# A transform, mix and two-MLP kernel: a buffer each for normalised, turned and read-back tokens, with chunk sizes, preparations, read-backs, decode pieces and the first channel transforms in another order

## The chip, the core and the metric

The kernel runs on one NeuronCore of a Trainium2 chip. Time is device time in microseconds (us) of one execution; lower is better. The engines are PE (TensorE, matrix products), DVE (VectorE), ACT (ScalarE), POOL (GpSimd) and SP (SyncE, which here only issues DMAs, one after the other, in one queue that keeps its order). Each engine runs its own instructions in order; semaphores tie the engines together.

## What is computed

Two sequences of 3136 tokens with 256 channels go through three layers. Cut to what matters:

```python
# 1: filter along the sequence
X  = rfft(x, axis=1)
Yr = Xr @ w_r - Xi @ w_i + b_r;  Yi = Xr @ w_i + Xi @ w_r + b_i
Y  = soft_threshold(Yr, 0.01) + 1j * soft_threshold(Yi, 0.01)
x  = irfft(Y, axis=1)
# 2: MLP1 (256 -> 1024 -> 256)
xn = (x - mean(x)) / sqrt(var(x) + 1e-6) * g_ln
x  = x + relu(xn @ w_ch1) @ w_ch2
# 3: Fourier mixing, then MLP2 of the same size with weights of its own
u  = x + real(fft(fft(x, axis=1), axis=2))
un = (u - mean(u)) / sqrt(var(u) + 1e-6)
out = u + relu(un @ w2_ch1) @ w2_ch2
```

## The kernel before

Every product is made of split operands: a value is taken apart into a high and a low part, and two or three matmuls of `fp32r` add up to one product (`mm3r`, lines L223 to L225).

**Layer 1.** Forward transforms, the channel product per frequency (`p2_mix`, L483) and the inverse transform. The last part of the inverse (class `Inverse`) runs in 16 steps per sequence: DVE turns a piece (L321), PE multiplies it (L323), ACT copies it out of PSUM into `yg` (L205). After the sixteenth step of a sequence seven DMAs write `yg` to `dY` in memory (L329, L331), and the token loads of MLP1 read it back (L595). The steps of the second sequence run as hooks inside the first chunks of MLP1.

**MLP1 and MLP2** are 13 chunks each, `mlp1[0..12]` and `mlp2[0..12]`, of up to four tiles of 128 tokens; chunks of sequence 0 come first. What one chunk needs, in its order:

- load: tokens from memory into `yb` (or, for the first ones, `u0r` or `stg`), L595;
- stats: mean and variance of each tile on DVE (L605, L606);
- norm: the root on ACT (L613), four small DVE operations (L614 to L617), then per tile two ACT passes (L627 subtracts the mean, L628 scales) into `yn`;
- flip: two DVE transposes of 32x32 blocks into `z` (L640), one DMA that writes `z` to `dT` in memory (L646) and one that reads it back channel by channel into `xt` (L649);
- trans: ACT and DVE split `xt` into the high and low operand in `u0r` (L664, L205, L213); `mlp1[0]` and `mlp1[1]` turn their tokens on PE instead (L672, split by L675 and L676);
- l1: for each of eight groups f of 128 hidden channels six matmuls (L223 to L225) into one of three PSUM buffers `psa`, which ACT empties with a relu (L690) and DVE with the low part (L692);
- l2: per tile 16 matmuls (L708, L709) into one of two buffers `psb`, two DVE additions (L712, L713) and a store (L721).

`yn`, `z` and `xt` all come from one pool "q" of three buffers that goes round in order of request: whoever asks next gets the buffer that was asked for three requests ago, and waits for its last reader.

**Layer 3's transform** stands between the two MLPs. Stage 4 (`Stage98`, matmuls on L223 to L225 into `psc`, ACT copies out, POOL L372 to L374, L213, L427) reads `dX` (L353), and writes `dA` (L428) in 16 steps per sequence: those of sequence 0 run as hooks in MLP1's chunks 8 to 10, those of sequence 1 in MLP2's chunks 1 to 3. The channel transform of an MLP2 chunk (class `Front`) loads pieces of `dA` (`r<-dA`, L756, L758), multiplies them (`stage_b`, L772), and `dmix` (from L797 on) adds the result to the token tile. `mlp2[6]` is the first that needs sequence 1 of `dA`.

**The order of the work.** `run_mlp` walks through the chunks. Around chunk k it puts, at numbered places ("l1" behind group f, "l2" behind tile i), the preparation of the next chunks: trans of k+1, stats, norm and flip of k+2, the loads of k+3 at its end, and the hooks: inverse steps, stage 4 steps, and eight pieces in which DVE decodes MLP2's weights (`MLP2_AT`). The tables at the head of the file give the places. On top of this a scheduler orders the instructions of each engine by durations of its own, within what the data allow, so that work can stand earlier or later than its place. Each DMA also waits for the DMA eight issues before it, since eight semaphores are used in turn.

Of the kernel before, what the change touches and what calls it, by code (L numbers as in the profile page):

```python
# [9 lines left out]
F32 = mybir.dt.float32  # L10
# [15 lines left out]
MLP2_AT = ((4, 6), (5, 2), (5, 6), (6, 2), (6, 6), (7, 3), (11, 2), (11, 6))  # L26
# [11 lines left out]
TRANS_AT = (0, 0)  # L38
# [18 lines left out]
D = 256  # L57
# [108 lines left out]
def fourier_moe_kernel(ctx, tc, x, w_r, w_i, b_r, b_i, g_ln, w11, w12, w21, w22,  # L166
# [415 lines left out]
    class Chunk:  # L582
# [3 lines left out]
        def __init__(self, nt, loads, stores, wv, g, front=None):  # L586
            self.nt, self.loads, self.stores, self.wv, self.g, self.front = nt, loads, stores, wv, g, front
            self.by_act = False
            self.flipped = True

        def load(self):
            self.y = next(y_ring).rearrange("p (i c) -> p i c", c=D)
# [3 lines left out]
            if self.front is not None:  # L596
                self.front.load()
# [10 lines left out]
        def norm(self):  # L608
# [9 lines left out]
            self.yn = qslot(F32).rearrange("p (i c) -> p i c", c=D)  # L618
# [15 lines left out]
        def flip(self, h):  # L634

            x = self.nt * 32
            if h == 0:
                self.z = qslot(F32)
# [9 lines left out]
            self.xt = qslot(F32)  # L648
# [3 lines left out]
        def trans(self, c):  # L652
            nt = self.nt
            n = nt * 128
            if c == 0:
                self.xh, self.xl = ((next(x_ring) if self.flipped else qslot()).rearrange("p (k c) -> p k c", k=2)
                                    for _ in range(2))
# [57 lines left out]
        def store(self, last):  # L715

            for ps_, i, n, ap in self.stores:
                if i + n - 1 != last:
                    continue
                s = self.o[ps_, i:i + n, :]  # L720
                sp.dma_start(out=ap, in_=s if n > 1 else s[:, 0, :])  # L721
# [3 lines left out]
    def chunks1(b, wv):  # L725
        cs = []
        if b == 0:
            plan = [(c * 512, 4) for c in range(6)]
        else:
            plan = [(64, 2), (320, 2)] + [(576 + c * 512, 4) for c in range(5)]  # L730
        for k, (r0, nt) in enumerate(plan):
            lo = [(ALLP, 0, nt, rows(dY[b], r0, 128, nt))]
            st = [(ALLP, 0, nt, rows(dX1[b], r0, 128, nt))]
            if b == 1 and k == 0:
# [182 lines left out]
    for i in range(NS + INV_BEHIND):  # L917
# [9 lines left out]
        if i == PREP0_AT[0]:  # L927
            with tc.high_priority(offset=100):
# [3 lines left out]
        if i == PREP0_AT[1]:  # L932
            for c in range(2):
# [4 lines left out]
    def run_mlp(chunks, nxt, hooks):  # L938

        allc = chunks + nxt  # L940
        for k, ch in enumerate(chunks):
# [3 lines left out]
            def put(part, i, f, *a):  # L945
# [5 lines left out]

            if n is not None and n.flipped:
                for c in range(2):
                    put("l2", TRANS_AT[c], split, c)
# [3 lines left out]
            for n_ in todo:  # L958
                if n_ is None:
                    continue  # L960
                two = n_.front is not None
                if two:
                    i = 0
                    for p, pr in enumerate(n_.front.pairs):
                        put("l1", STAGE_B_AT[p], n_.front.stage_b, p)
                        put("l1", DMIX_AT[p], n_.front.dmix, p, n_.y, i)
                        w = 2 if pr[0][1] else 1
                        for t in range(w):
                            put("l1", STATS2_AT[p], n_.stats, i + t)
                        i += w  # L970
                else:
                    def stats(t, ch=ch, n_=n_):
                        with ExitStack() as es:
                            if ch is mlp1[0]:
                                es.enter_context(tc.issue_after(ch.rest[STATS1_AT[t]]))
                            n_.stats(t)

                    for t in range(4):
                        put("l1", STATS1_AT[t], stats, t)
                put("l1", NORM_AT[two], n_.norm)  # L980
                if n_.flipped:
                    for h in range(2):
                        put("l2", FLIP_AT[h], n_.flip, h)
                else:
                    for c in range(2):
                        put("l2", ch.nt - 1, n_.trans, c)
# [9 lines left out]
            if far is not None:  # L996
                far.load()

    u0 = cp.tile([128, 8192], F32R, tag="u0", name="u0r")
    x_ring = ring(u0[:, 4096:8192], 4, 1024)  # L1000
# [94 lines left out]
```

## Time and profile before

| | |
|---|---|
| time, median of 3 runs | 821.51 us (818.88 to 823.38) |
| the profiled execution | 819.17 us, span 817.4 us |
| PE busy | 791.3 us (97%), 4276 matmuls |
| PE weight loads (beside the matmuls) | 658.9 us |
| DVE busy | 538.9 us (66%) |
| ACT busy | 364.1 us (45%) |
| POOL busy | 120.2 us (15%) |
| DMA | 95.16 MB, mean 116 GB/s |
| granted PE clock | 0.992 |

A line of the timeline gives start, duration, engine, line, operation, output <- input, how many instructions in a row it stands for, and in brackets the idle time of the engine before it and what ended it. Matmuls overlap, so their durations are longer than their distance. A window line gives an engine's busy time with its number of instructions, the granted PE clock (1.00 is full speed), and the share and rate of the DMA engines. The time of the profiled execution is 1.77 us longer than its span.

### The profile page before, as it was taken

What the parts mean: (1) busy time and instruction counts of PE and PEld (TensorE: products, weight loads), DVE (VectorE), ACT (ScalarE), POOL (GpSimd) and SP (SyncE); (2) the same over time, 40 slices, a digit from 0 to 9 for tenths busy, and PEclk for the clock granted to TensorE, in tenths of its full rate; (3) what the DMA queues carried; (4) which work ended last, traced back from release to release, by engine and by line L of the source; (5) the groups of instructions that cost most, each with busy time, mean ns of one, the idle gap of its engine ahead of it and who ended that gap; (6) DMA issues with size and microseconds to landing.
All of it is one profiled execution on the core that took longest, in us unless ns stands there. A gap on an engine that the chain in (4) does not pass through costs nothing.

```text
span 817.4 us, 12025 instructions
## 1 busy us (share of the span) xinstructions
PE 791.3 (97%) x4276; PEld 658.9 (81%) x4276; DVE 538.9 (66%) x1260; ACT 364.1 (45%) x791; POOL 120.2 (15%) x152
## 2 busy tenths in 40 slices
PE   9999999998999999989999999999979999999996
PEld 3888977966777888978788888888768898888885
DVE  6589996478557568976756874646535666666543
ACT  1422356356764444364442563555533444444321
POOL 1212221220000000025420002555300000000000
PEclk9999999999999999999999999999989999999999
DMA  8742200621177123464544135455352344322201
GB/s 231 218 134 86 78 1 2 211 105 54 51 226 218 65 78 129 163 167 150 172 163 129 64 105 155 137 157 165 100 142 78 101 137 122 93 67 79 69 23 33
DMA packets 79663, 95.16 MB, mean 116 GB/s; under 512 B 16610, under 2 KB 58858, under 8 KB 79408
## 3 DMA queue, kind: packets, MB, share of 16 engines
q1 hardware_dynamic: 79604, 94.40, 37.8%
q8 instruction: 34, 0.56, 0.3%
q14 instruction: 25, 0.20, 0.1%
HBM read 56.89 MB, written 37.49 MB: 115 GB/s over the span
## 4 chain that ended last, share of the span: by engine, by line
PE 76%; DMA 9%; DVE 8%; ACT 3%; SPq 2%; issue 1%; POOL 1%; ACTq 0%; POOLq 0%
PE psb L708 20%; PE psb L709 10%; PE psa L223 10%; PE psa L224 10%; PE psa L225 9%; PE psb L483 4%; PE psc L772 3%; PE psc L323 2%; PE psc L304 2%; PE psc L503 2%; PE psc L797 1%; DMA cb<-in_cb_dram 1%; PE psa L451 1%; DMA h<-in_x_dram 1%; DMA r<-dA 1%
## 5 line engine op out<-in xcount | busy, mean ns | idle before, releaser
L690 ACT ACTIVATE h<-psa 128x512 fp32r<-128x512 f32 (+2 forms) x208 | 116.3, 570 | 199.8 <-PE psa L225 157.0
L692 DVE SCALAR_TENSOR_TENSOR h<-psa,h 128x512 fp32r<-128x512 f32 (+2 forms) x208 | 134.4, 654 | 91.5 <-ACT h L690 89.9
L708 PE MATMUL psb<-r3a,h 128*128 128x512 f32 x392 | 137.5, 399 | 0.6 <-DVE o L713 0.6
L708 PE MATMUL psb<-r2b,h 128*128 128x512 f32 x392 | 137.7, 398 | 0.0
L709 PE MATMUL psb<-r2b,h 128*128 128x256 f32 x392 | 106.0, 281 | 0.0
L709 PE MATMUL psb<-r3a,h 128*128 128x256 f32 x392 | 105.9, 282 | 0.0
L483 PE MATMUL psb<-wm,h 128*128 128x256 f32 (+1 forms) x600 | 88.8, 298 | 0.9 <-DVE w L489 0.9
L708 PEld LDWEIGHTS psb<-r3a,h 128*128 128x128 f32 x392 | 71.6, 188 | 16.8 <-issue 1.5
L708 PEld LDWEIGHTS psb<-r2b,h 128*128 128x128 f32 x392 | 71.9, 188 | 14.7
L483 PEld LDWEIGHTS psb<-wm,h 128*128 128x128 f32 (+1 forms) x600 | 76.1, 189 | 8.7 <-issue 8.2
L223 PE MATMUL psa<-u0r,r2b 128*128 128x512 f32 (+2 forms) x208 | 81.9, 394 | 0.0
L224 PE MATMUL psa<-u0r,r2b 128*128 128x512 f32 (+2 forms) x208 | 80.0, 385 | 0.0
L225 PE MATMUL psa<-u0r,r2b 128*128 128x512 f32 (+2 forms) x208 | 79.6, 384 | 0.0
L709 PEld LDWEIGHTS psb<-r3a,h 128*128 128x128 f32 x392 | 73.7, 189 | 4.5 <-issue 0.7
L709 PEld LDWEIGHTS psb<-r2b,h 128*128 128x128 f32 x392 | 73.9, 189 | 3.2
L712 DVE TENSOR_TENSOR o<-psb,yb 128x256 f32<-128x256 f32 x74 | 30.6, 422 | 69.2 <-PE psb L709 68.4
L223 PE MATMUL psa<-u0r,r3a 128*128 128x512 f32 (+2 forms) x176 | 67.1, 382 | 4.0 <-DVE h L692 4.0
L205 ACT ACTIVATE yg<-psc 98x512 f32<-98x512 f32 (+2 forms) x58 | 48.4, 863 | 47.2 <-PE psc L503 27.2
L224 PE MATMUL psa<-u0r,r3a 128*128 128x512 f32 (+2 forms) x176 | 66.2, 376 | 0.0
L225 PE MATMUL psa<-u0r,r3a 128*128 128x512 f32 (+2 forms) x176 | 63.8, 380 | 0.0
L213 POOL TENSOR_TENSOR h<-w 128x512 f32<-128x512 f32 (+1 forms) x26 | 34.1, 1314 | 109.9 <-DVE w L490 76.4
L225 PEld LDWEIGHTS psa<-u0r,r2b 128*128 128x128 f32 x208 | 40.0, 192 | 7.7
(125 smaller groups left out, 1306.7 us busy)
## 6 DMA issues: line engine op xcount, KB each, us to landing
dT<-q SPq DMA_DIRECT2D x20, 512.0 KB
q<-dT SPq DMA_DIRECT2D x20, 512.0 KB
s<-in_moe_w_ch_dram SPq DMA_DIRECT2D x16, 512.0 KB
r<-dX SPq DMA_DIRECT2D x32, 196.0 KB
dA<-o SPq DMA_DIRECT2D x32, 196.0 KB
dY<-yg SPq DMA_DIRECT2D x12, 512.0 KB
r<-dA SPq DMA_DIRECT2D x48, 128.0 KB
dX<-o SPq DMA_DIRECT2D x11, 512.0 KB
```

Of the source, the lines that this page charges most:

```text
L205: nc.scalar.activation(out=o, in_=i, func=AF.Copy, scale=scale)
L213: ins = eng.tensor_tensor(out=o, in0=a, in1=b, op=ALU.subtract)
L223: nc.tensor.matmul(out=ps, lhsT=lh, rhs=rh, start=first, stop=False)
L224: nc.tensor.matmul(out=ps, lhsT=ll, rhs=rh, start=False, stop=False)
L225: ins = nc.tensor.matmul(out=ps, lhsT=lh, rhs=rl, start=False, stop=last)
L483: nc.tensor.matmul(out=ps[0:m, u * D:(u + 1) * D], lhsT=xv[:, o:o + m], rhs=wm_hl[wv][:, e, c, :], start=k == 0, stop=k == 11)
L690: ins = nc.scalar.activation(out=h[:, 0:n], in_=ps[:, 0:n], func=AF.Relu)
L692: ins = nc.vector.scalar_tensor_tensor(out=l[:, 0:n], in0=ps[:, 0:n], scalar=0.0, in1=h[:, 0:n], op0=ALU.max, op1=ALU.subtract)
L708: nc.tensor.matmul(out=ps, lhsT=h[:, ts_], rhs=w2[:, f, :], start=f == 0, stop=False)
L709: nc.tensor.matmul(out=ps[:, 0:D], lhsT=l[:, ts_], rhs=w2[:, f, 0:D], start=False, stop=f == NF - 1)
L712: nc.vector.tensor_tensor(out=o, in0=ps[:, 0:D], in1=self.y[:, i, :], op=ALU.add)
L772: nc.tensor.matmul(out=ps, lhsT=self.raw[p][0:n, k, q * 128:(q + 1) * 128], rhs=self.cols(n, pr[k][1], im), start=True, stop=True)
```

## The change

1. `yn`, `z` and `xt` have a fixed buffer each (`q_tiles[0..2]`) instead of the next one of the pool; the pair of operands of `mlp1[0]` and `mlp1[1]` moves from the pool to `u0r`.
2. The read-back `q<-dT` is a step of its own, `land`: for `mlp1[2]` and MLP2's chunks it comes in the next chunk behind l1 group 3, and on SP behind the last store of the chunk before; for the other chunks of MLP1 (`EARLY`) behind l2 tile 2.
3. Chunk sizes of MLP1, in tiles: before 4,4,4,4,4,4 and, for sequence 1, 3 (two plus a half of each sequence),2,4,4,4,4,4; after 4,4,4,4,2,4,3 and 4,4,4,4,4,4.
4. Stats, norm and flips of MLP1 chunks are put earlier; the channel transforms and preparations of `mlp2[0]` and `mlp2[6]` later (`LATE`); the decode piece of chunk 7 goes to chunk 12; the token loads of chunk k+3 come at the start of chunk k instead of its end (except `mlp1[6]`'s).

No arithmetic is added or taken away.

```diff
-MLP2_AT = ((4, 6), (5, 2), (5, 6), (6, 2), (6, 6), (7, 3), (11, 2), (11, 6))
+MLP2_AT = ((4, 6), (5, 2), (5, 6), (6, 2), (6, 6), (11, 2), (11, 6), (12, 3))
-STAGE_B_AT = (1, 3)
-DMIX_AT = (3, 5)
-STATS1_AT = (0, 1, 2, 3)
-STATS2_AT = (4, 6)
-NORM_AT = (4, 7)
-FLIP_AT = (1, 2)
+EARLY = {"stats": (("l1", 0), ("l1", 0), ("l1", 1), ("l1", 1)), "norm": ("l1", 2), "flip": (("l1", 5), ("l1", 6)),
+         "land": ("l2", 2)}
+LATE = {"b": (4, 6), "mix": (6, 7), "stats": (("l1", 7), ("l2", 0)), "norm": ("l2", 0), "flip": (("l2", 2), ("l2", 3))}
+LAND_AT = ("l1", 3)
...
-            self.yn = qslot(F32).rearrange("p (i c) -> p i c", c=D)
+            self.yn = q_tiles[0].rearrange("p (i c) -> p i c", c=D)
...
             if h == 0:
-                self.z = qslot(F32)
+                self.z = q_tiles[1]
...
-            self.xt = qslot(F32)
+            self.d = d
+
+        def land(self):
+            x, d = self.nt * 32, self.d
+            self.xt = q_tiles[2]
             sp.dma_start(out=self.xt[:, 0:8 * x].rearrange("p (i x) -> p i x", i=8),
                          in_=bass.AP(d.tensor, d.offset, [[x, 128], [128 * x, 8], [1, x]]))
...
-            plan = [(c * 512, 4) for c in range(6)]
+            plan = [(0, 4), (512, 4), (1024, 4), (1536, 4), (2048, 2), (2304, 4), (2816, 2)]
         else:
-            plan = [(64, 2), (320, 2)] + [(576 + c * 512, 4) for c in range(5)]
+            plan = [(64 + c * 512, 4) for c in range(6)]
...
             if n is not None and n.flipped:
+                if not n.landed:
+                    put(LAND_AT, land, n, allc[k - 1].sent if k else None)
...
+                    pl = LATE if n_ in (mlp2[0], mlp2[6]) else USUAL
...
+            soon = far is not None and far is not mlp1[6]
+            if soon:
+                far.fetch()
```

What the scheduler makes of it is seen at three places. In these rows an engine's instructions stand in their order; L numbers of the changed kernel are a few lines off those before.

DVE, end of MLP1's chunk 0, before: the end of the transposed preparation of `mlp1[1]` (L676), the additions of chunk 0's tiles (L712, L713), and the low parts `h` of chunk 1's l1 groups (L692).

```order
L676 SCALAR_TENSOR_TENSOR q<-psc,g_sb,q 128x512
L712 TENSOR_TENSOR o<-psb,stg 128x256
L713 TENSOR_TENSOR o<-psb,o 128x256
L321 STREAM_TRANSPOSE t_2107<-yg_85 128x512
L692 SCALAR_TENSOR_TENSOR h<-psa,h 128x512 x2
```

The same place now: L643 is the flip, two transposes for a chunk; the first pair is that of `mlp1[2]`, the second that of `mlp1[3]`.

```order
L683 SCALAR_TENSOR_TENSOR u0r<-psc,g_sb,u0r 128x512
L643 STREAM_TRANSPOSE q<-q 128x4x4x32 x2
L719 TENSOR_TENSOR o<-psb,stg 128x256
...
L719 TENSOR_TENSOR o<-psb,stg 128x256
L720 TENSOR_TENSOR o<-psb,o 128x256
L643 STREAM_TRANSPOSE q<-q 128x4x4x32 x2
L699 SCALAR_TENSOR_TENSOR h<-psa,h 128x512 x2
```

The flip of `mlp1[3]` has come ahead of chunk 1's low parts, and those of `mlp1[4]` and `mlp1[5]` follow between them; all write the one `z`, so each waits until the DMA of the one before has read it.

PE, MLP1's chunk 1, before: the sixteenth inverse step of sequence 1 (L323) stands behind three l1 groups of chunk 2 and ahead of the l2 of chunk 1's tiles 2 and 3.

```order
L225 MATMUL psa<-u0r,r3a 128x512 x3
L323 MATMUL psc<-t_2493,cim 98x512
L708 MATMUL psb<-r3a,h 128x512
L709 MATMUL psb<-r3a,h 128x256
```

Now it is the second L322 of these rows, with the fifteenth ahead of it; the rows above them are the end of two tiles' l2 and one l1 group of the next chunk.

```order
L715 MATMUL psb<-r3a,h 128x512
L716 MATMUL psb<-r3a,h 128x256
L222 MATMUL psa<-u0r,r3a 128x512
...
L224 MATMUL psa<-u0r,r3a 128x512
L322 MATMUL psc<-t_2333,cim 98x512
L322 MATMUL psc<-t_2475,cim 98x512
```

The last two inverse steps have moved behind 32 matmuls of l2 and six of l1.

SP, MLP2's chunk 2 to 3, before: `r_5863` is the last input of stage 4.

```order
L646 DMA dT_1657<-q 128x2x512
L428 DMA dA_71<-o_1661 98x512
L595 DMA yb<-dX_68 64x256
L721 DMA out_dram<-o 64x256 x2
L649 DMA q<-dT_1657 128x8x128
L595 DMA yb<-dX_69 64x256
L595 DMA yb<-dX_69 128x1x256
L721 DMA out_dram<-o 2x64x256
L428 DMA dA_71<-o_1661 98x512
L353 DMA r_5863<-dX_69 98x512
```

The same place now, where the last input is `r_5816`.

```order
L649 DMA dT_1657<-q 128x2x512
L427 DMA dA_71<-o_1661 98x512
L600 DMA yb<-dX_68 64x256
L728 DMA out_dram<-o 64x256 x2
L600 DMA yb<-dX_69 64x256
L600 DMA yb<-dX_69 128x1x256
L728 DMA out_dram<-o 2x64x256
L427 DMA dA_71<-o_1661 98x512
L656 DMA q<-dT_1657 128x8x128
L352 DMA r_5816<-dX_69 98x512
```

The read-back has moved behind two token loads, a store and a write of `dA`, and still stands ahead of the last input. On PE the first matmuls of `mlp2[6]`'s `stage_b` stand where they stood, behind the l2 of two tiles and nine matmuls of l1.

## Rows read from the trace of the kernel before

**Rows 1.** Waits of PE: line, releaser, us in total, times, longest.

```profile
PE psc L772 <- DMA r<-dA: 4.8, 2, 4.3
PE psa L223 <- DVE h L692: 4.0, 4, 1.9
PE psc L672 <- ACT yg L205: 2.4, 1, 2.4
PE psc L225 <- POOL u0r L213: 1.7, 1, 1.7
...
PE psc L218 <- POOL mhl L213: 0.5, 1, 0.5
PE psc L217 <- POOL mhl L390: 0.5, 1, 0.5
```

**Rows 2.** Windows: start:end, length, PE, PEld, DVE, ACT, POOL, PEclk, DMA, GB/s.

```profile
300.00:320.00 20.00, 20.00 (x104) 17.04 (x104) 15.54 (x31) 7.96 (x16) 0.00 (x0) 1.00 0.29 107
...
440.00:460.00 20.00, 20.00 (x113) 17.31 (x112) 19.50 (x58) 10.47 (x25) 0.00 (x0) 1.00 0.16 55
...
600.00:620.00 20.00, 15.67 (x71) 13.00 (x69) 5.95 (x12) 4.49 (x9) 0.00 (x0) 0.83 0.53 155
```

**Rows 3.** Timeline of ACT, end of chunk 0.

```profile
189.51 4.33 ACT L628 ACTIVATE q<-q,sm 128x256 f32<-128x256 f32 x8 [0.22 <-DVE sm L617]
```

**Rows 4.** Timeline of SP: two writes of dT and their read-backs.

```profile
195.60 0.39 SPq L646 DMA_DIRECT2D dT<-q  x1
198.55 0.37 SPq L649 DMA_DIRECT2D q<-dT  x1
...
252.77 0.48 SPq L646 DMA_DIRECT2D dT<-q  x1
260.79 0.37 SPq L649 DMA_DIRECT2D q<-dT  x1
```

**Rows 5.** Timelines of ACT and PE around 240 and 264 us.

```profile
239.10 1.31 ACT L627 ACTIVATE q<-u0r,ng 128x256 f32<-128x256 f32 x3 [3.54 <-issue]
...
242.87 0.50 PE L223 MATMUL psa<-u0r,r3a 128*128 128x512 f32 x1 [1.88 <-DVE h L692]
...
264.18 0.50 PE L223 MATMUL psa<-u0r,r3a 128*128 128x512 f32 x1 [0.81 <-DVE h L692]
```

**Rows 6.** Timelines of ACT, SP and DVE: sequence 1 of dY and its loads.

```profile
231.35 1.10 ACT L205 ACTIVATE yg<-psc 98x512 f32<-98x512 f32 x1 [0.59 <-PE psc L323]
...
243.33 1.45 SPq L649 DMA_DIRECT2D q<-dT  x1
...
253.79 1.08 DVE L605 BATCH_NORM_STATS2 st<-yb 128x6 f32<-128x256 f32 x3 [3.53 <-DMA yb<-dY]
...
258.21 0.43 DVE L605 BATCH_NORM_STATS2 st<-yb 128x6 f32<-128x256 f32 x1 [0.21 <-DMA yb<-dY]
```

**Rows 7.** Timeline of PE, first l1 groups of MLP1's chunk 8.

```profile
361.04 0.50 PE L223 MATMUL psa<-u0r,r3a 128*128 128x512 f32 x1 [1.16 <-DVE h L692]
```

**Rows 8.** Timelines of SP, POOL, ACT and PE: end of stage 4.

```profile
576.50 0.39 SPq L649 DMA_DIRECT2D q<-dT  x1
...
578.89 2.58 SPq L428 DMA_DIRECT2D dA<-o  x1
581.57 0.72 SPq L353 DMA_DIRECT2D r<-dX  x1
...
589.05 0.73 POOL L372 TENSOR_TENSOR w<-r 98x254 f32<-98x254 f32 x1 [11.46 <-DMA r<-dX]
...
593.67 1.70 ACT L628 ACTIVATE q<-q,sm 128x256 f32<-128x256 f32 x4
595.26 1.06 ACT L205 ACTIVATE o<-psc 98x512 f32<-98x512 f32 x2
...
604.25 1.05 SPq L756 DMA_DIRECT2D r<-dA  x2
...
610.41 1.08 PE L772 MATMUL psc<-cb,r 128*128 128x64 f32 x4 [4.33 <-DMA r<-dA]
```

More of the change, by code (lines that the diff above doesn't have):

```diff
@@ L589, in __init__, with fetch @@
             self.flipped = True
+            self.landed = False
         def load(self):
+            self.fetch()
+            if self.front is not None:
+                self.front.load()
+        def fetch(self):
             self.y = next(y_ring).rearrange("p (i c) -> p i c", c=D)
@@ L655, in trans @@
             if c == 0:
-                self.xh, self.xl = ((next(x_ring) if self.flipped else qslot()).rearrange("p (k c) -> p k c", k=2)
+                self.xh, self.xl = (next(x_ring).rearrange("p (k c) -> p k c", k=2)
                                     for _ in range(2))
@@ L720, in store @@
                 s = self.o[ps_, i:i + n, :]
-                sp.dma_start(out=ap, in_=s if n > 1 else s[:, 0, :])
+                ins = sp.dma_start(out=ap, in_=s if n > 1 else s[:, 0, :])
+                self.sent = getattr(ins, "ins", ins)
     ALLP = slice(0, 128)
@@ L727, in chunks1 @@
         if b == 0:
[L728 removed]
+            plan = [(0, 4), (512, 4), (1024, 4), (1536, 4), (2048, 2), (2304, 4), (2816, 2)]
         else:
[L730 to L731 removed]
+            plan = [(64 + c * 512, 4) for c in range(6)]
+        for r0, nt in plan:
             lo = [(ALLP, 0, nt, rows(dY[b], r0, 128, nt))]
             st = [(ALLP, 0, nt, rows(dX1[b], r0, 128, nt))]
[L734 removed]
+            if r0 == 2816:
                 for src, lst in ((dY, lo), (dX1, st)):
@@ L927, in fourier_moe_kernel @@
         if i == PREP0_AT[0]:
+            q_tiles = [qslot(F32) for _ in range(3)]
             with tc.high_priority(offset=100):
@@ L943, in run_mlp, with put @@
             at = {}
-            def put(part, i, f, *a):
+            def put(when, f, *a):
+                part, i = when
+                if part == "n":
+                    carry.append((("l1", i), f, a))
+                    return
                 at.setdefault((part, min(i, ch.nt - 1) if part == "l2" else i), []).append(lambda: f(*a))
@@ L950, in split, with land @@
                     n.trans(c)
+            def land(n, back):
+                with ExitStack() as es:
+                    if back is not None:
+                        es.enter_context(tc.issue_after(back))
+                    n.land()
+            for when, f, a in carried:
+                put(when, f, *a)
+            carried, carry = [], []
             if n is not None and n.flipped:
+                if not n.landed:
+                    put(LAND_AT, land, n, allc[k - 1].sent if k else None)
                 for c in range(2):
-                    put("l2", TRANS_AT[c], split, c)
+                    put(("l2", 0), split, c)
             todo = [m]
@@ L996, in run_mlp @@
             if far is not None:
-                far.load()
-    u0 = cp.tile([128, 8192], F32R, tag="u0", name="u0r")
-    x_ring = ring(u0[:, 4096:8192], 4, 1024)
+                if not soon:
+                    far.fetch()
+                if far.front is not None:
+                    far.front.load()
     dT = [dp.tile([2, 65536], F32, name=f"dT{i}") for i in range(3)]
```

34 lines of the change are left out of this document (20 added, 14 removed).

## The prediction

> **What bounds the kernel now.** The page's first part comes first: PE is busy 97% of the span, and the time is that of its matmuls plus what PE waits. The change takes no matmul away, so it can only move waits. The waits of PE are read next [rows 1]: the reader is to see how short the list is, and that every entry belongs to one of four places. One is the transposed preparation of `mlp1[1]` (2.4, L672). The second is the l1 groups of the following chunks (L223, 4.0 in four waits). The third is the end of sequence 0's stage 4 input (0.5 and 0.5, L217 and L218, with 1.16 of L223 just behind). The fourth is the end of stage 4 of sequence 1 (1.7 and 4.3, L225 and L772). Windows say the same: 20.00 of 20 us where nothing is missing, 15.67 in 600:620, with a granted clock of 0.83 there [rows 2]. The clock's two levels are 1.2 and 2.4 GHz, so 0.83 over 20 us means 6.8 us at the lower one, which costs 3.4 us beside the wait itself. The average share of the other engines (DVE 66%) says nothing here; each place is read from its own chain.
>
> From 300:320 comes a price that serves below: 104 matmuls in 20 us without a gap, 0.19 us each in the mix of l1 and l2 [rows 2].
>
> **Chunks 0 to 3 of MLP1.** The 2.4 us at L672 are a wait for ACT's copy of `yg`, which stood behind eight L628 in one go, 4.33 us [rows 3], because the norms of two chunks ran together. In the changed order only `mlp1[1]`'s norm stands ahead of these transposes, since `yn` is one buffer and `mlp1[2]`'s norm has to wait for them. That takes four L628 (2.2 us) and four L627 of 0.44 (1.8 us, by the three of 1.31 in [rows 5]) from the chain: 4.0, more than the wait. It goes: -2.4.
>
> In chunks 2 and 3 a norm stood at the head of ACT, waiting for a "q" buffer that a DMA was still reading, with the relus queued behind it: ACT idle 3.54 ahead of L627, then PE idle 1.88, later 0.81 [rows 5]. With buffers of their own and norms put early this waiting goes: -1.88 -0.81, and 0.15 for the fourth of L223's waits (4.0 less 1.88, 0.81 and the 1.16 of [rows 7]). Together with L672: -5.2.
>
> Two things come in. First, one `z`: the flips of `mlp1[3]`, `[4]` and `[5]` stand on DVE ahead of or between chunk 1's low parts, each waiting until the write of the flip before has read `z`. PE waits for the low parts, since they empty `psa`. A write took 2.95 us by the issue of the read-back behind it (195.60 to 198.55) [rows 4]. Ahead of the first of these waits lie a norm (four times 0.44 and 0.54, 3.9) and that write, 6.9 us and two flips on top; PE has meanwhile 32 matmuls of l2 and three l1 groups, 50 times 0.19, 9.6 us. So it is nearly covered; the later two have only what PE holds in three buffers (18 times 0.19, 3.5) against the same 2.95 and the work between. The bounds are 0 and three whole writes, 8.9. I take 2.
>
> Second, the last inverse step of sequence 1 moves behind 32 matmuls of l2 and six of l1, 38 times 0.19, 7.3 us. PE gets there 0.4 earlier (2.4 less 2), so the last copy of `yg`, 231.35 before [rows 6], comes at about 238.2. Behind it SP writes `dY` and loads the tokens of the next chunks. One thing that stood between goes, the read-back at 243.33 of 1.45 us; the tokens come 5.5 us later. Before, DVE waited 3.53 for the first of these (253.79) and had the third load at 258.21 [rows 6]; now that is about 263.7. In the changed order the statistics of three of these chunks stand on DVE ahead of chunk 3's first low part, and those are not done before 265. PE would have been at the fourth l1 group at 263.4 (264.18 less 0.81, [rows 5]), now 2.4 earlier, at 261. That makes a wait of 4, and one more when the last load follows: 5. Bounds: 0, if the writes go faster without the other traffic, and 8, the shift of 5.5 and the 2.4 that PE is ahead. The sum of this place: -5.2 +2 +5 = +1.8, from -5.2 to +11.7.
>
> **Chunks 6 to 8.** The middle of sequence 0's stage 4 input still follows chunk 6 (three tiles in both). Chunk 7 has four tiles instead of two, so PE has more work ahead of L217: two tiles of l2 alone are 32 times 0.19, 6.1 us, against waits of 0.5, 0.5 and then 1.16 [rows 1, 7]. -2.2; bounds 0 and -2.2. What is next late there is nothing that I can see.
>
> **Decode pieces.** One goes from chunk 7 to 12, beside MLP2's first preparations. In the window that holds two pieces DVE was busy 19.50 of 20, and PE lost nothing (20.00) [rows 2]. Chunk 12 becomes as full; half a microsecond of slack is no cover for a late load. +0.5, between 0 and 3. The shorter wait of L772 (4.8 less 4.3 [rows 1]) may go with the later place of `mlp2[0]`'s transforms: -0.3, between 0 and -0.5.
>
> **End of stage 4.** SP stood at the read-back until 576.50, then issued token loads, a store, a write of `dA` that held it from 578.89 on, and only then, at 581.57, the last `r<-dX`; POOL began on it at 589.05 after 11.46 idle [rows 8]. From that came PE's 1.7 and, behind ACT's copies of 595.26, the late `dA`, the loads at 604.25 and the 4.33 at 610.41. Now the loads and the store go ahead of the read-back, but the write of `dA` too, which waits for the DMA eight before it, about the same `dT` write. So the gain is between 0 and 5.1 (581.57 less 576.50); I take 3, the half of it that the loads and the store make. The last input is there at 586, the 1.7 goes. ACT then has its norm (L628, 593.67) behind it earlier and copies 1 us sooner: the loads at about 600.3, PE on L772 at 606.4 instead of 610.41. PE itself is there 1.7 earlier than the 606.1 of before, so it still waits 2 us and the clock falls as it did. -4 for the whole place; bounds 0 and -9.4 (1.7, 4.3 and the 3.4 of the clock). That `LATE` puts `stage_b` later gives nothing, because its first matmuls stand on PE where they stood. The token loads that move to a chunk's start cost nothing: SP issues one in some 0.4 us and mostly waits; if that cover goes, they are in the bounds.
>
> **Sum.** +1.8 -2.2 +0.5 -0.3 -4 = -4.2 against the profiled execution's 819.17 (1.77 above its span): 815.0. The median of the runs shown, 821.51, is 2.3 higher, so measured medians may well come out a little above the sum too.
>
> **Rivals.** A: no change. The chain through `dY` gives back 8 instead of 5, and SP's write of `dA` holds the last input so that the last place gains 1 instead of 4: 819.17 -4.2 +3 +3 = 821. For it speaks that the inverse step did move by 7.3 us and that PE's order at `mlp2[6]` did not change; against it that less traffic lies between.
>
> B: every named wait goes. -5.2 -2.2 -0.5 -9.4 = -17.3: 802. For it speaks that each edit stands at one of the four places; against it the inverse step and the same place of L772.
>
> C: slower, by the single `z`. The flips of `mlp1[6]` to `[9]` follow each other on DVE in chunk 3, ahead of low parts, while the loads and writes of `dY` are on the way. There a write was not read back before 8.0 us (252.77 to 260.79) [rows 4]. Each flip then waits 8.0 for its predecessor, against 3.5 of work in three buffers and 9.6 where two tiles of l2 come between; at 3 us a flip, four of them cost 12: 819.17 -4.2 +12 = 827. It decides as soon as a write takes longer than some 6 us. Against it: behind the loads there is nothing else to write there. The Trainium skill (DMA: Bandwidth & Descriptors, section "Latency and other measured facts") puts the access latency of HBM at 0.2 us on average and 2 us at high load; an estimate by that page makes the write under load 4.8 us, mostly covered, and C then costs nothing. The two waits shown [rows 4] differ by 5.1 us and not 1.8; so the trace does not agree, if all of the 8.0 is the write, and C keeps its chance.
>
> **How the numbers follow.** Forecast (810 to 818) 0.42, A 0.26, B 0.12, C 0.20. The range 803 to 825 takes in the forecast, A and the inner edge of B, and leaves out C's 827 and B's 802. The likeliest case's own range is 810 to 818. About 0.5% (4.1 us) is what a measurement of this kernel tells from no change. Faster by more than that, below 817.4: B and nine tenths of the forecast, 0.50. Slower, above 825.6: C, 0.20. Between: 0.30.
>
> **What would show it.** Right: no wait of L672 near 192, no L223 wait near 242; a new wait of PE for DVE of 1 to 3 us in chunk 1 and of 4 to 6 in chunk 3, with DVE's statistics idle ahead of it for `yb<-dY`; no waits on L217 and L218; POOL's last L372 about 3 us earlier against the work around it, no wait on L225, and a wait of 1 to 4 us on L772 for `r<-dA`. Wrong: chunk 3 without a wait (B's half), or DVE idle before L640's successor for `dT` over 3 us several times (C), or L772's wait as long as before (A).

## The result and the profile after

The changed kernel takes 824.62 us (median of 18 runs, 821.90 to 829.35) against 819.34 for the kernel before (18 runs on the same chip): a ratio of 1.0066, with a 95% interval of 1.0048 to 1.0084. (One run of the kernel before took 2776.05 us; the ratio leaves it out.) It is 5.3 us slower. The forecast was 815.0, faster; the time lies inside the range of 803 to 825, at its upper edge, and the sign was wrong.

The profiled execution of the changed kernel is one of its fastest, 821.94 (span 820.0), so a second profile of the same kernel was taken; it is one of the slowest, 829.59 (span 827.6). Below, "after" is the first and "after, again" the second. A place counts as changed where both profiles agree.

Waits of PE in the changed kernel: line, releaser, us in total, times, longest. These answer to [rows 1]; the lines are those of the changed kernel (L772 is L780 now, L223 is L222, L672 is L679).

```profile
PE psa L222 <- DVE h L699: 7.5, 8, 2.6
PE psc L780 <- DMA r<-dA: 6.9, 2, 3.5
PE psa L222 <- DVE w L207: 1.7, 1, 1.7
PE psc L222 <- DVE mv L609: 1.3, 1, 1.3
```

As forecast, the wait of L672 for ACT's `yg` is down from 2.4 to 0.3, and those of stage 4 for POOL (L217, L218, L225) are gone. The l1 groups wait longer (7.5 against 4.0), and the wait for `r<-dA` comes twice at some 3.5 where it came once at 4.3 and once at 0.4. Windows of the same kernel say where (columns as in [rows 2]):

```profile
240.00:260.00 20.00, 18.43 (x96) 15.47 (x95) 9.78 (x33) 7.25 (x17) 0.00 (x0) 1.00 0.73 239
260.00:280.00 20.00, 17.07 (x91) 14.15 (x92) 14.04 (x46) 16.41 (x42) 0.00 (x0) 1.00 0.35 126
380.00:400.00 20.00, 18.65 (x89) 14.43 (x87) 13.60 (x32) 5.56 (x15) 10.08 (x11) 1.00 0.60 190
500.00:520.00 20.00, 16.61 (x84) 13.95 (x83) 6.14 (x16) 7.90 (x18) 10.54 (x18) 0.91 0.48 123
580.00:600.00 20.00, 17.98 (x91) 14.04 (x90) 12.44 (x33) 9.96 (x24) 9.80 (x14) 1.00 0.34 106
600.00:620.00 20.00, 16.52 (x77) 13.70 (x76) 7.73 (x15) 5.91 (x13) 0.57 (x3) 0.91 0.50 141
```

The stretch 600:620 is better than before (16.52 and 0.91 against 15.67 and 0.83 in [rows 2]); 500:520 is the new hole.

To compare kernels whose work is shifted in time, the lost time of PE was worked out from each trace: for each pair of successive matmuls, the time from start to start less the median of that kind (line and shape) in the same kernel, summed by stretch. It holds waits and lower clock alike. The span less this loss is 785.0 to 786.7 us in all fifteen traces, so the table accounts for the differences between spans. (The three small matmuls of the middle step, L216 to L218, come twice each, and the median of two shares a wait behind one of them between two stretches. In a_r3 one such interval is 2.65 us, so its row is worked out with 0.09 for L218, as in the others; elsewhere this shifts a figure by less than 0.4.)

```
us lost by PE    0-160 160-330 330-380 380-440 440-560 560-640  640-   all
before            2.9    10.8     2.7     0.7     0.9    12.2    0.5   30.7
after             3.2    12.5     1.4     2.1     5.6     9.1    0.6   34.4
after, again      5.4    12.2     0.7     4.4     6.8    11.7    0.6   41.8
b_sizes           3.2    13.1     6.3     2.3     1.1    11.3    0.8   38.1
a_sizes           2.8    10.3     0.9     0.1     7.5     8.9    0.6   31.0
a_dec             3.8    12.4     6.6     0.9     6.3    10.3    0.7   40.8
a_ring            4.7    12.5     1.3     2.0     7.7     9.5    0.7   38.4
a_inv2            2.9    15.0     0.9     3.7     5.5     8.8    0.6   37.3
a_r3              4.0    12.8     0.7     1.2     5.4     9.9    0.5   34.5
as_r3             6.5    13.8     1.2     0.1     9.1     9.0    1.9   41.6
a_pin             4.7     7.6     6.3     4.1     7.8     9.3    0.7   40.3
as_pin            5.7     5.9     4.0     0.7     7.0     8.7    0.6   32.5
b_pin             5.9    10.8     6.4     5.0     1.4    11.0    0.7   41.2
a_ud              4.5    12.6     5.4     0.3     1.9    13.6    0.6   39.0
as_pin_d6         5.7     6.0     3.6     2.0     1.2    10.0    0.6   29.0
```

The rows below the third are the experiments' (a_ stands on the changed kernel, b_ on the one before, as_ on the changed kernel with the old chunk sizes). The first 160 us hold nothing that was changed and vary by up to 3.7 us from one execution to the next; with single profiles, a difference of 1 or 2 us elsewhere says little by itself.

### The profile page after: what moved, and what is told of

The parts are those of the page before. It is cut to its first block, busy times and chain, and to the rows that moved or that the text cites. A ratio compares the mean times of both kernels' runs of the same rounds, so it can differ in the third digit from the quotient of the medians.

```text
span 820.0 us, 12035 instructions
## 1 busy us (share of the span) xinstructions
PE 789.9 (96%) x4276; PEld 656.4 (80%) x4276; DVE 543.0 (66%) x1260; ACT 363.3 (44%) x791; POOL 124.2 (15%) x152
## 4 chain that ended last, share of the span: by engine, by line
PE 64%; DMA 12%; DVE 11%; SPq 4%; ACT 4%; issue 2%; POOL 1%; DVEq 0%; ACTq 0%; POOLq 0%
PE psb L715 17%; PE psb L716 9%; PE psa L222 8%; PE psa L223 8%; PE psa L224 8%; PE psb L482 4%; DMA yb<-dY 3%; PE psc L780 2%; SPq L328 2%; PE psc L303 2%; PE psa L450 2%; DVE st L608 2%; PE psc L322 2%; PE psc L502 2%; DMA dA<-o 1%
## 5 line engine op out<-in xcount | busy, mean ns | idle before, releaser
L222 PE MATMUL psa<-u0r,r3a 128*128 128x512 f32 (+2 forms) x208 | 83.6, 403 | 7.3 <-DVE h L699 7.2
L222 PE MATMUL psa<-u0r,r2b 128*128 128x512 f32 (+2 forms) x208 | 81.7, 393 | 1.9 <-DVE w L207 1.7
L223 PE MATMUL psa<-u0r,r2b 128*128 128x512 f32 (+2 forms) x208 | 79.3, 381 | 0.0
L223 PE MATMUL psa<-u0r,r3a 128*128 128x512 f32 (+2 forms) x208 | 78.7, 379 | 0.0
L224 PE MATMUL psa<-u0r,r3a 128*128 128x512 f32 (+2 forms) x208 | 75.8, 380 | 0.1
L222 PEld LDWEIGHTS psa<-u0r,r3a 128*128 128x128 f32 x208 | 39.1, 188 | 20.0 <-DVE h L699 12.4
```

The lines of the kernel that those rows point to most:

```text
L222: nc.tensor.matmul(out=ps, lhsT=lh, rhs=rh, start=first, stop=False)
L223: nc.tensor.matmul(out=ps, lhsT=ll, rhs=rh, start=False, stop=False)
L224: ins = nc.tensor.matmul(out=ps, lhsT=lh, rhs=rl, start=False, stop=last)
```

## The experiments

All ratios are to the kernel before, timed on the same chip, with their 95% intervals.

**First set: which part, and is it the buffers?** P stands for places (the new waits come from where the instructions stand), B for the fixed buffers, S for a cost spread over the kernel. The changed kernel once more:

> The changed kernel once more, as a second sample of its waits. Theory P (places): its trace shows the same three new waits as the first one, some 4.5 us of PE for DVE near 258 to 268, 3.4 for r<-dA near 505 with a fall of the clock behind it, 1.3 near 398, and the ratio to the kernel before is 1.005 to 1.008. Theory B (buffers: the single z, yn and xt make the preparation serial) expects the same ratio, with waits of DVE for dT writes. Theory S (spread: the clock falls more often and no place can be named) expects the waits at other places than in the first trace.

825.47 us, 1.0068 [1.0046, 1.0089]. The result holds, and the waits come at the same places (2.55 at 266.17, 2.17 at 401.45, 4.65 at 513.49), as P said; S, which expected other places, falls.

The fixed buffers back to the pool:

```diff
-            self.yn = q_tiles[0].rearrange("p (i c) -> p i c", c=D)
+            self.yn = qslot(F32).rearrange("p (i c) -> p i c", c=D)
-                self.z = q_tiles[1]
+                self.z = qslot(F32)
-            self.xt = q_tiles[2]
+            self.xt = qslot(F32)
```

> The changed kernel with yn, z and xt from the pool of three again (the operands of the first two chunks stay in u0r, the places stay). Theory B: the loss was the single buffers, so 4 us or more less, ratio at most 1.002. Theory P: the three new waits stay, ratio 1.005 to 1.008 or more, since a norm may again wait for a buffer that a DMA reads. Theory S: any.

824.53, 1.0051 [1.0035, 1.0067]: no faster than the changed kernel beyond the intervals, where B expected at most 1.002. The wait of L679 on `yg` comes back (1.60 us), so the fixed buffers did remove it; B falls, though a part of the 5 us below the noise is not excluded.

The decode table of before:

```diff
-MLP2_AT = (..., (6, 6), (11, 2), (11, 6), (12, 3))
+MLP2_AT = (..., (6, 6), (7, 3), (11, 2), (11, 6))
```

> The changed kernel with the decode piece back in chunk 7. The scheduler then puts the first channel transform of mlp2[3] back behind twelve l1 matmuls, 3.5 us of PE work later, as before. Theory P: the wait of 3.4 for r<-dA near 505 shrinks to under 1 and the 1.7 us of clock behind it go, so 4 to 5 us less than the changed kernel, ratio 1.000 to 1.002. Theories B and S: within 1 us of the changed kernel, 1.0055 to 1.0075.

826.52, 1.0071 [1.005, 1.0092]: no gain, where P expected 4 to 5 us. The wait for `r<-dA` is gone from there, as P said, but the hole near 500 stays in another form: PE waits 3.11 for DVE's addition (L720) at 517.73, because DVE had stood 7.18 for ACT's `sm` (L616), and ACT 5.89 for POOL's `w`. And a new one came at sequence 0's middle step (3.68 at 346.85).

The chunk sizes of before:

```diff
-            plan = [(0, 4), (512, 4), (1024, 4), (1536, 4), (2048, 2), (2304, 4), (2816, 2)]
+            plan = [(c * 512, 4) for c in range(6)]
-            plan = [(64 + c * 512, 4) for c in range(6)]
+            plan = [(64, 2), (320, 2)] + [(576 + c * 512, 4) for c in range(5)]
```

> The changed kernel with the chunk sizes of before. The last inverse step then stands 7 us of PE work earlier, as before. Theory P: the waits near 258 to 268 shrink from 4.5 to 1 or less, those on the middle step near 350 to 360 (2 us in the kernel before) may come back; the r<-dA wait near 505 stays: 2 to 4 us less than the changed kernel, ratio 1.002 to 1.004. Theory B: no gain, 1.006. Theory S: any.

821.19, 1.0006 [0.9989, 1.0023]: 4.3 us faster than the changed kernel, level with before. That is more than P expected (1.002 to 1.004). In time the sizes carry nearly all of the loss, although the hole at 440–560 is still there (7.5); the other edits together are then worth about nothing, gains at 185–380 (3.1) and 560–640 (3.4) against that hole (6.6 more than before).

**Second set: what in the sizes, and the late load.** D stands for the chain through `dY` as set by the inverse step's place, Z for the sizes by themselves, L for the late load ahead of L780, K for the view that what follows that load is as late as itself. The new sizes alone, on the kernel before (the a_sizes diff, reversed):

> The kernel before with the chunk sizes of the changed one and nothing else. On PE the last inverse step stays where it was. Theory D: no loss, and the waits on the middle of stage 4's input near 350 to 360 (2.2 us) may go: ratio 0.996 to 1.001. Rival Z: the sizes cost as they do in the changed kernel, 4 us: ratio at least 1.004.

824.93, 1.0058 [1.0036, 1.008]. By themselves they cost what the whole change costs: Z holds. The largest part (6.3 us lost at 330–380, 2.7 before) is seen at sequence 0's middle step. These are rows of this kernel's timeline (start us, us, engine, line, operation, tiles; in brackets the idle time before and what ended it), and the window around them:

```profile
338.67 1.12 SPq L721 DMA_DIRECT2D dX<-o  x2
341.96 0.96 SPq L385 DMA_DIRECT2D m<-dX  x1
346.24 0.27 POOL L390 CAST mhl<-m 98x32 fp32r<-98x32 f32 x1 [177.64 <-DMA m<-dX]
346.57 0.34 PE L217 MATMUL psc<-mhl,ca_hl 98*98 98x32 f32 x1 [3.34 <-POOL mhl L390]
340.00:360.00 20.00, 16.66 (x72) 13.67 (x71) 12.85 (x33) 8.82 (x23) 3.62 (x6) 0.83 0.29 72
```

The same in the kernel before:

```profile
345.24 1.57 SPq L721 DMA_DIRECT2D dX<-o  x2
348.77 0.97 SPq L385 DMA_DIRECT2D m<-dX  x1
352.96 0.77 POOL L390 CAST mhl<-m 98x32 fp32r<-98x32 f32 x1 [184.35 <-DMA m<-dX]
353.78 0.26 PE L217 MATMUL psc<-mhl,ca_hl 98*98 98x32 f32 x1 [0.49 <-POOL mhl L390]
```

With the new sizes sequence 0 ends two tiles earlier, so its last store comes 6.6 us earlier (338.67 against 345.24) and POOL has the middle mode about as much earlier (346.24 against 352.96). But PE's step was placed earlier still: PE was at it at 343.23 against 353.29 (each start less its wait), so it waited 3.34 instead of 0.49, and the clock fell to 0.83. The chain store, load, POOL takes 7.6 and 7.7 us, about the same.

Two more inverse steps put ahead of MLP1:

```diff
-STAGE3_END = 3
+STAGE3_END = 5
-              (2, 0), (2, 1), (2, 2), (2, 3), (3, 0))
+              (2, 0), (2, 1), (2, 2))
```

> The changed kernel with two more of sequence 1's inverse steps done before MLP1 (five instead of three), so that the last one stands on PE 18 us of work earlier than in the changed kernel and 11 earlier than before; chunk sizes, buffers and places stay. Theory D (the chain through dY): the waits of PE for DVE near 258 to 268, 4.0 to 4.5 us, shrink to under 1, and the kernel takes 3 to 5 us less than the changed one: ratio to before 1.001 to 1.003. Rival Z (the sizes themselves: a two-tile chunk gives the next preparation too little time): those waits or others in chunks 3 to 5 stay, ratio at least 1.005.

827.31, 1.0082 [1.0051, 1.0113]: no faster than the changed kernel, where D expected the waits of chunk 3 to go. The tokens do come earlier, but the scheduler moves their statistics forward as well. Rows of this kernel:

```profile
242.51 0.43 DVE L608 BATCH_NORM_STATS2 st<-yb 128x6 f32<-128x256 f32 x1 [5.84 <-DMA yb<-dY]
246.12 0.80 PE L222 MATMUL psa<-u0r,r3a 128*128 128x512 f32 x1 [5.81 <-DVE h L699]
```

DVE stands for a load as before, 12 us earlier and longer. D falls: the place of the inverse step does not decide it. That the place of the statistics against their load does is put to the test in the third set.

The load of MLP2's chunk 3 issued at the start of chunk 0 instead of its end:

```diff
+            ahead = far is mlp2[3]
+            if ahead:
+                far.front.load()
...
-                if far.front is not None:
+                if far.front is not None and not ahead:
```

> The changed kernel with the loads of mlp2[3]'s transform pieces issued at the start of mlp2[0] instead of its end, so that they stand on SP ahead of the middle load of stage 4, which waits for the last store of MLP1. Theory L (the load is late behind that wait): the wait for r<-dA near 505 goes, with it the fall of the clock, 3 to 6 us less than the changed kernel, ratio 1.000 to 1.003. Rival K (what follows there is as late, as the wait of 3.1 us for the additions of l2 in the kernel with the old decode table): another wait of 2 us or more between 500 and 520, within 2 us of the changed kernel.

824.12, 1.005 [1.0029, 1.0071]. The wait for `r<-dA` near 508 is gone, and PE waits 2.41 for ACT's copy of `u0r` at 509.27 instead; the loss at 440–560 is 5.4, as before this edit (5.6): K, and not L's 3 to 6 us. The same with the sizes of before:

> The changed kernel with the chunk sizes of before and the early loads of mlp2[3]. Theories D and L together: the early loss and the wait near 505 both go, ratio 0.993 to 0.997, below the kernel before. Rivals Z or K: ratio 0.999 to 1.003.

823.58, 1.0039 [1.0018, 1.006], not faster than a_sizes: a miss for D and L together. Its profile, taken of its slowest run (828.64), has a wait of 5.5 for `r<-dA` and one of 6.0 at sequence 1's middle step (L216). It settles nothing more.

**Third set: the statistics.** T says that the statistics, placed by the scheduler ahead of the landing of their loads, block DVE, and that placing them later frees PE. The edit holds the statistics of four chunks behind the chunk's own low parts:

```diff
-                            if ch is mlp1[0]:
+                            if ch is mlp1[0] or n_ in mlp1[6:10]:
```

> The changed kernel with one order held: the statistics of mlp1[6] to [9], sequence 1's first chunks, may not be scheduled ahead of the chunk at whose place they are written (they then stand on DVE about two chunks ahead of their use instead of all four in chunk 3); sizes, buffers and every other place stay. Theory T (DVE stands at statistics for tokens that have not landed, with the low parts that PE needs queued behind): the waits of 4.0 to 4.5 us near 258 to 268 go to under 1, those near 297, 398, 505 and 610 stay; 3 to 4.5 us less than the changed kernel, ratio 1.001 to 1.003. Rival Z (the sizes cost wherever the work stands): other waits of 3 us or more come up in chunks 3 to 8, ratio at least 1.005.

825.74, 1.0065 [1.0042, 1.0088]. The waits at 258 to 270 are gone (230–285 loses 0.1 instead of 5.4), as T said, and no time is gained, as Z said: PE comes earlier to the middle step and waits there, with this row, and it loses more again up to 560.

```profile
343.39 0.26 PE L216 MATMUL psc<-mhl,ca_hl 98*98 98x32 f32 x1 [4.15 <-POOL mhl L389]
```

With the sizes of before:

> The changed kernel with the chunk sizes of before and the same order held. With these sizes the statistics of all four chunks stood in chunk 3 too, and PE waited 2.0 near 247 with the clock at half for 3.4 us behind it and 0.45 near 255. Theory T: these go, 3 to 4.5 us less than the kernel with the sizes alone, ratio 0.995 to 0.997. Rival Z: ratio 1.000 or more.

818.93, 0.997 [0.9951, 0.9988]. Here the gain is kept: the middle step comes 0.95 late and not 4.15. On the kernel before:

> The kernel before with the same order held and nothing else. Theory T: DVE's idle of 3.5 us at the statistics near 254 goes and with it the waits of PE of 0.6 near 255 and 0.8 near 264; the 1.9 near 242, which comes from a norm that waits for its buffer, stays: 1 to 1.5 us less, ratio 0.998 to 0.999, at most barely to be told from none. Rival Z: no change, or slower by a later preparation.

827.44, 1.0084 [1.0061, 1.0108], a miss for T. The waits near 255 and 264 are gone, as T said, but the kernel waits more at 344 to 440 (5.9 us in all against 2.2) and 6.2 instead of 4.3 for `r<-dA` at the end of stage 4. This kernel's preparation still takes its buffers from the pool of three; whether that is why was not tested. T is right on the place and no rule for the whole.

**Fourth set: the passage from MLP1 to MLP2.** X says that decode table and `LATE` together set the order around PE's L780 near 505, so that PE and the norm of `mlp2[2]` meet the late load; Y that the read-back step and the buffers do. Both undone:

```diff
-MLP2_AT = (..., (6, 6), (11, 2), (11, 6), (12, 3))
+MLP2_AT = (..., (6, 6), (7, 3), (11, 2), (11, 6))
-                    pl = LATE if n_ in (mlp2[0], mlp2[6]) else USUAL
+                    pl = USUAL
```

> The changed kernel with the decode table of before and without LATE (all of MLP2 by USUAL). In the order of the instructions ACT then has the norm of mlp2[2] seven relus ahead of stage 4's first copies, as in the kernel before; with either edit alone the norm stands between or behind them. Theory X (the passage from MLP1 to MLP2, 440 to 560 us: a norm behind copies that wait for a late load): PE's loss there, 5.6 to 6.8 us, falls to 1.5 or less. But with the piece back in chunk 7 and these sizes the middle step of stage 4 stands 7 us of PE work earlier, and a wait for m<-dX of 3.5 to 4 us with the clock at half behind it comes back near 343. Together: within 2 us of the changed kernel, ratio 1.003 to 1.007. Rival Y (the single buffers or the later read-back cause the loss there): it stays at 5 or more, ratio 1.010.

825.85, 1.0069 [1.0044, 1.0095]. The hole at 440–560 goes from 5.6–6.8 to 1.9 (X said 1.5 or less, Y 5 or more), with buffers and read-back unchanged: X holds for the place and Y falls. Since a_dec, which undoes the decode table alone, keeps the hole (6.3), `LATE` has a part in it; `LATE` was not undone alone, so whether the table has one too is open. The total does not move, because with this table the middle step stands where it waits (5.4 at 330–380), and the end of stage 4 without `LATE` for `mlp2[6]` loses 13.6. So the last run takes the sizes and the decode table of before, the pinned statistics, and `LATE` for `mlp2[6]` alone:

```diff
-                    pl = LATE if n_ in (mlp2[0], mlp2[6]) else USUAL
+                    pl = LATE if n_ is mlp2[6] else USUAL
```

> The changed kernel with the chunk sizes of before, the statistics of mlp1[6] to [9] held at their places, the decode table of before, and LATE for mlp2[6] alone. Theory X: the loss between 440 and 560 us, 6.95 in the kernel with sizes and statistics alone, falls to 1.5 or less, and the middle step keeps its place, so 4 to 6 us less than that kernel: ratio to before 0.989 to 0.993, faster than both. Rival Y: ratio 0.996 to 0.999 as there.

816.87 us, 0.9961 [0.9941, 0.998]: faster than the changed kernel and the one before, 3.1 us below the median of the latter on that chip. The loss at 440–560 falls to 1.2, as X said, but the ratio lies where Y had it (0.996 to 0.999) and not where X did (0.989 to 0.993). Its window at 500, and below it that of as_pin:

```profile
500.00:520.00 20.00, 19.79 (x112) 16.81 (x111) 8.04 (x20) 6.48 (x15) 10.50 (x18) 1.00 0.51 123
```

```profile
500.00:520.00 20.00, 16.49 (x77) 13.79 (x76) 5.96 (x13) 6.15 (x14) 10.52 (x18) 0.83 0.56 145
```

The trace shows 3.5 us less lost time than as_pin's, 5.8 of it less at 440–560 and 1.3 each more at 380–440 and 560–640; of the ratios, 0.9961 against 0.997, the intervals overlap, so that the passage is worth 4 to 6 us in the median is not shown.

## Why the prediction was wrong, point by point

```
us of PE's lost time   forecast    after   after, again
chunks 0 to 3            +1.8      +1.7       +1.4
chunks 6 to 8            -2.2      -1.3       -1.9
380-440                   0        +1.4       +3.7
440-560                  +0.2      +4.7       +5.9
end of stage 4           -4        -3.2       -0.6
```

Each figure is the stretch's loss less that of before; chunks 0 to 3 are 160–330 and chunks 6 to 8 are 330–380. The column of forecasts sums to -4.2; the measured columns with 0–160 and the rest give +3.7 and +11.1, and the medians +5.3, between them.

**Chunks 0 to 3: right in sum, but one term only by luck.** The rows of the changed kernel's timeline:

```profile
212.38 0.45 DVE L643 STREAM_TRANSPOSE q<-q 128x256 f32<-128x256 f32 x1 [2.52 <-DMA dT<-q]
236.63 1.99 ACT L204 ACTIVATE yg<-psc 98x512 f32<-98x512 f32 x2 [0.26 <-PE psc L322]
238.64 8.62 SPq L328 DMA_DIRECT2D dY<-yg  x6
254.42 0.43 DVE L608 BATCH_NORM_STATS2 st<-yb 128x6 f32<-128x256 f32 x1 [4.77 <-DMA yb<-dY]
257.73 1.08 DVE L608 BATCH_NORM_STATS2 st<-yb 128x6 f32<-128x256 f32 x3 [0.47 <-DMA yb<-dY]
259.85 0.50 PE L222 MATMUL psa<-u0r,r3a 128*128 128x512 f32 x1 [1.57 <-DVE h L699]
264.06 0.50 PE L222 MATMUL psa<-u0r,r3a 128*128 128x512 f32 x1 [2.56 <-DVE h L699]
298.18 0.50 PE L222 MATMUL psa<-u0r,r3a 128*128 128x512 f32 x1 [0.96 <-DVE h L699]
```

They answer to [rows 3 to 6]. The 2.4 of L672 is down to 0.3, and the 1.88 and 0.81 are gone. The last copies of `yg` run from 236.63 to 238.6; the forecast had the last one start at about 238.2. PE waits 1.57, 2.56 and 0.36 (at 268.80), 4.5 in all, where 5 was forecast.

But the reason given for the 5, tokens that come 5.5 us later, did not come true. The last load that DVE stood for was there at 257.73, where 263.7 was forecast and 258.21 was measured before: SP was done with issuing the writes of `dY` in 9.9 us (238.64 to 248.53) instead of 13.6 before (232.48 to 246.04), which is the case that the prediction priced at 0. What PE waited for is the row of statistics that stands on DVE ahead of the low parts: DVE is idle 4.77 for the first tokens (3.53 before) and has then the statistics of all four chunks and the first flip to do. a_pin, which holds these statistics back, loses 0.1 at 230–285 where the changed kernel loses 5.4. So the number was met by luck.

The single `z` was overpriced: DVE waited 2.52 for the read of it, PE some 0.5, not 2. Rival C, which had `z` as the cause, falls with a slower result all the same; a_ring says so too. Of the flips of `mlp1[6]` to `[9]` that C names only the last, at 280.61, waited for `dT<-q`, 3.2 us where C had 8.0 for each, and PE did not wait there. The Trainium skill (DMA: Bandwidth & Descriptors, section "Latency and other measured facts") puts the access latency of HBM at 2 us at high load, from which the prediction estimated that C costs nothing. The trace agrees. A wait of 0.96 at 298, and one of 0.58 near 180, were not priced and fill up the sum.

**Chunks 6 to 8: the number right, its reason wrong.** I put the 2.2 down to the fourth tile of chunk 7. But a_sizes, which has chunk 7 of two tiles, loses only 0.9 there, and b_sizes, which has four, loses 6.3. The changed kernel escapes by where PE's order puts the step. Counted in PE's work from the start, without what it loses, its middle step stands at 332.7 us, against 325.6 to 325.8 in a_dec, a_ud, a_pin and b_sizes, which wait 3.3 to 4.2 there, and 338.2 before. The decode piece is one thing that moves it, since a_dec changes nothing else; but in a_pin, where the piece is not in that chunk either, holding the statistics back moves it as far.

**What is next late: not seen.** "What is next late there is nothing that I can see" was an oversight. Rows of the changed kernel, behind the middle step:

```profile
385.05 4.38 SPq L427 DMA_DIRECT2D dA<-o  x3
391.07 0.35 SPq L600 DMA_DIRECT2D yb<-dY  x1
397.61 1.40 DVE L608 BATCH_NORM_STATS2 st<-yb 128x6 f32<-128x256 f32 x4 [3.66 <-DMA yb<-dY]
399.48 0.44 PE L222 MATMUL psc<-u0r,ca_hl 98*98 98x512 f32 x1 [1.26 <-DVE mv L609]
```

A token load stands on SP behind three writes of `dA`, DVE's statistics stand for it 3.66, and PE 1.26 (2.17 in the second profile, with a clock of 0.91 behind it). Before, the load was issued at 387.09 instead of 391.07. With the old sizes 380–440 loses 0.1 (a_sizes). That the earlier end of sequence 0 pulls stage 4's work up against the last chunks of MLP1 is the likely reason and was not tested by itself; a_dec and a_ud, which have the new sizes but have waited at the middle step already, lose only 0.9 and 0.3.

**The failed step: the passage at 440–560.** The step of the sum that failed by most is "The shorter wait of L772 may go with the later place of `mlp2[0]`'s transforms: -0.3", with the +0.5 for the decode piece in chunk 12. The stretch lost 4.7 to 5.9 instead of 0.2. By the traces this alone uses up the forecast's 4.2; 380–440, priced at nothing, and the smaller gain at the end of stage 4 make the result slower. Rows of the changed kernel there:

```profile
494.27 0.79 SPq L728 DMA_DIRECT2D dX<-o  x1
501.75 0.91 SPq L384 DMA_DIRECT2D m<-dX  x1
505.21 1.77 SPq L764 DMA_DIRECT2D r<-dA  x4
...
504.76 0.28 PE L716 MATMUL psb<-r2b,h 128*128 128x256 f32 x1
508.43 0.66 PE L780 MATMUL psc<-cb,r 128*128 128x64 f32 x4 [3.39 <-DMA r<-dA]
...
508.76 0.64 ACT L204 ACTIVATE u0r<-w 98x512 fp32r<-98x512 f32 x1 [5.80 <-POOL w L373]
509.30 1.69 ACT L631 ACTIVATE q<-q,sm 128x256 f32<-128x256 f32 x4
511.02 1.30 DVE L643 STREAM_TRANSPOSE q<-q 128x512 f32<-128x512 f32 x2 [7.19 <-ACT q L631]
```

The same place in the kernel before:

```profile
493.51 0.41 SPq L721 DMA_DIRECT2D dX<-o  x1
500.68 0.92 SPq L385 DMA_DIRECT2D m<-dX  x1
504.24 1.78 SPq L756 DMA_DIRECT2D r<-dA  x4
...
504.01 0.28 PE L709 MATMUL psb<-r2b,h 128*128 128x256 f32 x1
504.13 0.39 PE L223 MATMUL psa<-u0r,r2b 128*128 128x512 f32 x1
...
506.65 0.39 PE L225 MATMUL psa<-u0r,r2b 128*128 128x512 f32 x1
507.47 1.35 PE L772 MATMUL psc<-cb,r 128*128 128x64 f32 x8 [0.43 <-DMA r<-dA]
```

From the issue of MLP1's last store to the moment that PE's wait for `r<-dA` ends, the changed kernel takes 14.2 us (494.27 to 508.43) and the one before 14.0 (493.51 to 507.47). The chain is about as long. What differs is PE: before, two groups of l1, 12 matmuls of 0.23 us, stand between the last l2 and L772; in the changed kernel none does, so PE arrives 10.8 us after the store (508.43 less 3.39 less 494.27) and not 13.5 (507.47 less 0.43 less 493.51). In a_ud and as_pin_d6, without `LATE` for `mlp2[0]` and with the decode table of before, the 12 matmuls stand there again, and PE waits 0.31 and 0.21. I read the later place of the channel transforms as room gained, and did not look at what the scheduler set free in front of L780. The lower clock (0.91 over 500:520) comes on top, and ACT's second half of the norm of `mlp2[2]` (L631) stands behind copies that wait for POOL, with DVE's flip behind it. That ACT and PE then wait for the same chain fits a_r3, which hurries one load and gains nothing there.

The time of the runs does not tie the 5.3 us to this passage alone: a_sizes keeps the hole and is level with the kernel before, and a_ud closes it and is not faster. What the runs show is that the prediction missed two things, this order in front of L780 and what the sizes cost; the sizes it had credited by name with 2.2 us, and by themselves they cost 5.5 (b_sizes). A part of its +5 for chunk 3 belongs to them too: with the old sizes PE waits 2.4 there (a_sizes).

**End of stage 4: the input earlier as forecast, the gain mostly by the clock.** Rows of the changed kernel that answer to [rows 8]:

```profile
586.22 0.40 SPq L656 DMA_DIRECT2D q<-dT  x1
586.71 2.60 SPq L352 DMA_DIRECT2D r<-dX  x1
587.09 0.50 PE L222 MATMUL psa<-u0r,r2b 128*128 128x512 f32 x1 [1.66 <-DVE w L207]
594.47 1.26 POOL L371 TENSOR_TENSOR w<-r 98x254 f32<-98x254 f32 x1 [5.96 <-ACT u0r L204]
614.54 1.26 PE L780 MATMUL psc<-cb,r 128*128 128x64 f32 x6 [3.48 <-DMA r<-dA]
```

The last `r<-dX` is issued 3.5 us earlier against PE's work (an estimate: 586.71 less the 26.6 that PE had lost by then, against 581.57 less 18.0), where 3 was forecast. POOL's last input no longer ends an idle time, and the wait on L225 (1.73 before) is gone; in its place PE waits 1.66 for DVE's small copy of `w` (L207), which was not in the sum. L780 waits 3.48 instead of 4.33, where 2 was forecast. The two waits together are 0.9 shorter; the rest of the 3.2 goes with the clock, 0.91 in 580:600 and 0.83 in 600:620 before, 1.00 and 0.91 now, of which the prediction said that it falls as it did. In the second profile the two waits are 3.0 and 3.8, and of the gain 0.6 is left.

What stays open: which of the new sizes costs the 4 to 5 us that the changed kernel loses at 285 to 440 beyond a_sizes (chunks 4 and 7 change size, and the tokens of those between them shift); why two profiles of one kernel differ by 7 us of lost time, of which 2.3 are in the unchanged first 160 us; and the 9 to 14 us at 560–640, which no version removed.

## What to carry to other kernels

A load at the end of a chain of fixed length (here store, load, load: 14 us) is to be compared with the work that the bound engine has queued between the same two points, in the order before and after; an edit that moves other instructions away from in front of the consumer shortens that cover though it touches neither load nor consumer. Price an edit of sizes by every point that is tied to the end of the resized piece, and undo it alone before crediting it with a gain: here the wait that it was credited with removing was absent without it (a_sizes). A wait removed on an engine that feeds such a chain is often handed on: pinning the statistics took 5 us out of one place and paid only together with the sizes that let the next place be on time.

## What was not expected of the hardware

Not every hole of PE is followed by the lower clock. Waits of 1.57 and 2.56 at 259.85 and 264.06 went with a granted clock of 1.00 in 240:260 and 260:280; one of 3.39 went with 0.91 (500:520), one of 3.51 with 0.83 (as_pin, same window), and a shorter one of 2.17 (second profile, 401.45) with 0.91 in 400:420. And a chain through memory is stiffer than its neighbours: from MLP1's last store to the end of PE's wait for the loads that hang on it was 13.8 to 14.9 us in the nine traces with a wait of 0.3 us or more there, while PE's own arrival moved by 3 us.
